# Transposing q by the DMA crossbar, and putting the two attention products of a tile into one burst on TensorE

## The chip, the cores and the metric

The kernel runs on one core of one Trainium2 chip. The metric is the device time of one execution in microseconds (us), as the median of several executions. The kernel before takes 288.21 us (median of 3 runs, 287.4 to 288.27). "Span" below is the time of one profiled execution between its first and its last instruction; it is about 2 us shorter than the device time.

Engine names in the profile: PE is TensorE (matmuls), PEld its weight loads, DVE is VectorE, ACT is ScalarE, POOL is GpSimd, SP is SyncE, which here does nothing but issue DMAs. A "q" after a name (SPq, ACTq) is that engine's instruction queue, as it issues DMAs.

## The reference, cut to what matters

```
q_s = softmax of q over the head dimension         # per row of q
k_s = softmax of k over the sequence               # per column of k
kv  = einsum('bhsd,bhse->bhde', k_s, v)            # k-v product, 64 x 64 per head
att = einsum('bhsd,bhde->bhse', q_s, kv)           # output product
x   = att as [batch * seq, heads * head_dim]       # 4608 x 512
h   = x @ w_in                                     # 512 -> 2048, first matrix product
out = leaky_relu(h) @ w_out                        # 2048 -> 512, second matrix product
```

There are 8 batches of 8 heads, 576 rows of sequence and 64 of head dimension. The two large products are almost all of the work. The kernel goes through x in 9 tiles of 512 rows, which I number 0 to 8. Tile t consists of the first product (64 matmuls of 128x512) and the second (another 64, in four quarters of 16). Attention is prepared ahead: during tile t the kernel finishes batch t+1 and starts on batch t+2.

## The kernel before

Only the parts that the change and the argument touch are shown; `...` marks cuts.

```python
ld_pool = ctx.enter_context(tc.tile_pool(name="ld", bufs=7))
ps_pool = ctx.enter_context(tc.tile_pool(name="ps", bufs=4, space=bass.MemoryType.PSUM))
# pair() takes one of only 4 PSUM tiles of two banks; every matmul result goes to one
...
qe_buf.append(const_pool.tile([P, NG, R * D], BF16, name=f"qe{i}"))     # i = 0, 1
...
def make_transpose(st, b, gp, r0=0, r1=R, copy=None, before=None):      # q on PE
    def piece():
        ...
        pt = pair("pt", BF16)
        for r in range(r0, r1):
            for par, g, lo, to in quads(gp):
                nc.tensor.matmul(
                    pt[to : to + HP, par, r * D : (r + 1) * D],
                    lhsT=qe_buf[b % 2][lo : lo + HP, g, r * D : (r + 1) * D],
                    rhs=ident[lo : lo + HP, lo : lo + HP],
                    is_transpose=True, ...)
        ...
        (copy or nc.vector.tensor_copy)(out=st["qT"][...], in_=pt[...])
...
def prep_pieces(b, st):
    return [
        make_exp(st, b, "q", 0),      # 0  exp on ACT
        make_qnorm(st, b, 0),         # 1  reduce, reciprocal, multiply on DVE
        make_exp(st, b, "q", 1),      # 2
        make_qnorm(st, b, 1),         # 3
        make_exp(st, b, "k", 0),      # 4
        make_exp(st, b, "k", 1),      # 5
        make_vcast(st, b, 0, NG),     # 6  v to bf16 on DVE
    ]
...
# slots: (1, j) runs after column block j (of 16) of the first product,
#        (2, s) after quarter s of the second product
elif t + 1 < B:
    st = states[t + 1]
    put((1, 2), [kv_piece(st, t + 1)] + transpose_pieces(t + 1, st))
    put((1, 8), out_pieces(t + 1))
if t + 2 < B:
    prep = prep_pieces(t + 2, states[t + 2])
    put((2, 0), prep[0:4])
    put((2, 1), prep[4:6])
    put((2, 2), prep[6:7])
...
for t in range(NT):
    if t > 0 and t + 2 < B:
        load_batch(nc.sync, t + 2)          # q, k and v of batch t+2, on SP
    emit_moe(t, slots_of(t))                # its stores are on SP too
```

The order in which these pieces are emitted is the order in which each engine executes its part of them; nothing reorders them later.

The softmax here doesn't subtract the row's maximum and nothing guards it: scores larger than these inputs give would overflow.

## Time and profile before

| | before |
|---|---|
| time, median | 288.21 us |
| span of the profiled run | 285.8 us |
| PE busy | 98% |
| one half of a tile (64 matmuls of 128x512) | 13.81 us, 216 ns each |
| transposes of one batch on PE, tiles 2 to 6 | 0.77 to 0.87 us |
| traffic of the loads falls off, from the start of tile 4 | 15.0 us |
| v's load complete, from the start of tile 2 | 16.7 us |

The first lines of the page, and its line on DMA packets:

```profile
span 285.8 us, 5509 instructions
PE 278.7 (98%) x2484; PEld 130.9 (46%) x2484; DVE 109.5 (38%) x145; ACT 118.8 (42%) x118; POOL 12.8 (4%) x23
...
DMA packets 21894, 42.29 MB, mean 148 GB/s; under 512 B 1776, under 2 KB 6640, under 8 KB 21872
```

PE is busy all the time, and no other engine over half of it. The chain of waits that ended last, in order of time, says the same and shows the pieces. These are its lines for tile 4 (start us, length us, what):

```profile
136.85 2.59 PE ph L376 x12
139.44 0.71 PE pkv L234 x71
140.15 0.77 PE pt L209 x72
140.92 5.29 PE ph L376 x24
146.21 0.61 PE po L280 x16
146.82 6.16 PE ph L376 x28
152.98 13.81 PE pout L385 x64
```

The tile of 29.94 us (136.85 to 166.79) is 27.85 us of the two large products and 2.09 us of attention: k-v product (pkv), transposes of q (pt), output product (po). There is no wait in it.

From the timeline of DVE in the second half of tile 4 (start, length, instruction, and in brackets the idle time before it and who ended it):

```profile
155.13 1.35 DVE L183 TENSOR_REDUCE qsum<-qe 128x18 f32<-128x1152 bf16 x1 [6.69 <-ACT qe L158]
...
158.09 1.34 DVE L183 TENSOR_REDUCE qsum<-qe 128x18 f32<-128x1152 bf16 x1
...
161.04 1.22 DVE L402 COPY out_sb<-pout 128x1024 f32<-128x1024 f32 x1
162.18 1.35 DVE L168 CAST vb<-v_ld 128x2304 bf16<-128x2304 f32 x1
```

Two normalizations of q (each a reduce, a reciprocal and a multiply, which take 2.95 us), then the copy that empties the first pair of output subtiles from PSUM (pout), then the cast of v, last. Roughly when v arrives is seen in the windows (columns: window, length, busy us and count of five engines, clock, DMA share, GB/s), where the load traffic of tile 4 falls off:

```profile
151.00:151.50 0.50, 0.50 (x4) 0.19 (x2) 0.00 (x0) 0.21 (x1) 0.00 (x0) 1.00 0.92 364
151.50:152.00 0.50, 0.50 (x4) 0.24 (x3) 0.00 (x0) 0.50 (x1) 0.00 (x0) 1.00 0.27 101
```

That is 15.0 us after the tile's start at 136.69, about 10 us before the cast that reads v. And these are the loads on SP's queue:

```profile
140.58 0.67 SPq L84 DMA_DIRECT2D q_ld<-in_q_dram  x1
141.34 0.55 SPq L84 DMA_DIRECT2D k_ld<-in_k_dram  x1
141.99 2.11 SPq L84 DMA_DIRECT2D v_ld<-in_v_dram  x1
```

They follow the stores of the tile before, 3.9 us after the tile's start.

### The profile page before, as it was taken

To read this page: it belongs to the slowest core of one execution; us is meant where nothing else is said; L and a number is where in the kernel's file an instruction comes from. 1 tells how busy PE (TensorE), PEld (TensorE's weight loads), DVE (VectorE), ACT (ScalarE), POOL (GpSimd) and SP (SyncE) were. 2 spreads that over 40 slices of the span, in tenths; PEclk is the share of its full clock that TensorE was granted. 3 is DMA by queue.
4 is the path that set the end of the run, shared out by engine and by line. 5 is a ranking of instruction groups with operands and counts; after the bars stand their busy time and mean duration, and the time that the engine had idled before them with its cause. 6 is when DMAs were issued, how large, how long until landed. Compare 5 with 4: busy or idle time off the path is not lost.

```text
span 285.8 us, 5509 instructions
## 1 busy us (share of the span) xinstructions
PE 278.7 (98%) x2484; PEld 130.9 (46%) x2484; DVE 109.5 (38%) x145; ACT 118.8 (42%) x118; POOL 12.8 (4%) x23
## 2 busy tenths in 40 slices
PE   8899999999999999999999999999999999999994
PEld 3344444444454445444544454444444444444443
DVE  2930385919822654246422833092311100110012
ACT  5646444891146703680268116731560065015400
POOL 0832200000000000000000000000000000000000
PEclk9999999999999999999999999999999999999999
DMA  7999999890398036902492149404200330032014
GB/s 260 309 200 246 346 346 402 254 363 5 73 254 320 1 73 152 399 23 66 97 393 92 29 103 337 181 0 99 50 2 0 73 76 0 5 81 63 0 32 114
DMA packets 21894, 42.29 MB, mean 148 GB/s; under 512 B 1776, under 2 KB 6640, under 8 KB 21872
## 3 DMA queue, kind: packets, MB, share of 16 engines
q1 hardware_dynamic: 15312, 30.55, 34.3%
q0 software_dynamic: 6400, 11.27, 15.3%
q8 instruction: 19, 0.31, 0.5%
q10 hardware_dynamic: 160, 0.13, 0.2%
q14 instruction: 3, 0.02, 0.0%
HBM read 36.70 MB, written 9.44 MB: 161 GB/s over the span
## 4 chain that ended last, share of the span: by engine, by line
PE 84%; DMA 13%; POOL 1%; DVE 0%; SPq 0%; issue 0%
PE ph L376 39%; PE pout L385 39%; DMA w_out_sb<-in_moe_w_out_dram 7%; DMA w_in_sb<-in_moe_w_in_dram 4%; DMA k_ld<-in_k_dram 2%; PE pkv L234 2%; PE po L280 2%; PE pt L209 1%; PE pout L414 1%; POOL w_in_sb L116 1%; SPq L84 0%; DVE xT L296 0%; DVE out_sb L422 0%; POOL gate L124 0%
## 5 line engine op out<-in xcount | busy, mean ns | idle before, releaser
L376 PE MATMUL ph<-xT,w_in_sb 128*128 128x512 bf16 x576 | 127.7, 379 | 0.0
L431 ACT ACTIVATE g_sb<-ph 128x1024 bf16<-128x1024 f32 x72 | 73.5, 1023 | 125.1 <-PE ph L376 125.1
L385 PE MATMUL pout<-w_out_sb,g_sb 128*128 128x512 bf16 x560 | 123.4, 379 | 0.3 <-DMA w_out_sb<-in_moe_w_out_dram 0.3
L376 PEld LDWEIGHTS <-w_in_sb 128*128 128x128 bf16 x576 | 55.2, 98 | 66.6 <-issue 1.2
L385 PEld LDWEIGHTS <-g_sb 128*128 128x128 bf16 x560 | 54.4, 98 | 65.8 <-issue 1.0
L402 DVE COPY out_sb<-pout 128x1024 f32<-128x1024 f32 (+1 forms) x18 | 21.4, 1192 | 78.9 <-PE pout L385 76.7
L183 DVE TENSOR_REDUCE qsum<-qe 128x18 f32<-128x1152 bf16 (+2 forms) x18 | 21.9, 1215 | 47.6 <-ACT qe L158 47.6
L296 DVE CAST xT<-po 128x128 bf16<-128x128 f32 (+7 forms) x23 | 13.7, 639 | 28.0 <-PE po L280 27.9
L185 DVE TENSOR_TENSOR qe<-qe,qrec 128x1152 bf16<-128x1152 bf16 (+2 forms) x18 | 22.0, 1225 | 0.6
L158 ACT ACTIVATE ke<-k_ld 128x1152 bf16<-128x1152 f32 x16 | 17.9, 1155 | 4.7 <-DMA k_ld<-in_k_dram 4.7
L158 ACT ACTIVATE qe<-q_ld 128x1152 bf16<-128x1152 f32 x16 | 17.9, 1156 | 3.7 <-DMA q_ld<-in_q_dram 3.7
L219 DVE COPY qT<-pt 128x1152 bf16<-128x1152 bf16 (+1 forms) x16 | 11.3, 740 | 1.1 <-PE pt L209 1.1
L152 PE MATMUL scr<-wsrc 128*128 128x512 bf16 x36 | 10.1, 440 | 1.2 <-DVE wsrc L92 1.2
L296 ACT CAST xT<-po 128x896 bf16<-128x896 f32 (+3 forms) x7 | 5.8, 829 | 12.5 <-PE po L280 12.5
L168 DVE CAST vb<-v_ld 128x2304 bf16<-128x2304 f32 (+2 forms) x8 | 9.6, 1199 | 0.0
L209 PE MATMUL pt<-ident,qe 64*64 64x64 bf16 x568 | 7.6, 196 | 0.5 <-DVE qe L185 0.5
L234 PE MATMUL pkv<-vb,ke 64*64 64x65 bf16 x576 | 6.7, 193 | 0.9 <-ACT vb L168 0.4
L234 PEld LDWEIGHTS <-ke 64*64 64x64 bf16 x576 | 5.7, 106 | 4.1 <-issue 3.3
L209 PEld LDWEIGHTS <-qe 64*64 64x64 bf16 x568 | 6.7, 104 | 1.5 <-issue 1.4
L280 PE MATMUL po<-qT,kd 64*64 64x512 bf16 (+7 forms) x128 | 6.4, 293 | 0.4 <-DVE kd L246 0.4
L152 PEld LDWEIGHTS <-wsrc 128*128 128x128 bf16 x36 | 3.7, 109 | 6.4 <-issue 2.7
L245 DVE RECIPROCAL krec<-pkv 128x4 f32<-128x4 f32 (+1 forms) x9 | 1.6, 178 | 11.2 <-PE pkv L234 11.1
(28 smaller groups left out, 40.1 us busy)
## 6 DMA issues: line engine op xcount, KB each, us to landing
out_dram<-out_sb SPq DMA_DIRECT2D x70, 128.0 KB, 2.4
q_ld<-in_q_dram SPq DMA_DIRECT2D x5, 1152.0 KB, 6.8
k_ld<-in_k_dram SPq DMA_DIRECT2D x5, 1152.0 KB, 8.8
v_ld<-in_v_dram SPq DMA_DIRECT2D x5, 1152.0 KB, 10.8
q_ld<-in_q_dram POOLq DMA_DIRECT2D x2, 1152.0 KB, 18.1
k_ld<-in_k_dram POOLq DMA_DIRECT2D x2, 1152.0 KB, 20.1
v_ld<-in_v_dram POOLq DMA_DIRECT2D x2, 1152.0 KB, 19.8
w_in_sb<-in_moe_w_in_dram POOLq DMA_DIRECT2D x3, 512.0 KB, 10.2
```

The costliest lines, as they stand in the source:

```text
L152: nc.tensor.matmul(scratch["t"][:, 0, :], lhsT=wsrc[:, 0:P], rhs=wsrc, start=True, stop=True)
L158: nc.scalar.activation(out=(qe_buf if nm == "q" else ke_buf)[b % 2][:, 2 * gp : 2 * gp + 2, :], in_=st[nm][:, 2 * gp : 2 * gp + 2, :], fun ...
L183: nc.vector.reduce_sum(out=qsum[:, :, 0:n], in_=x, axis=AX.X)
L185: nc.vector.tensor_tensor(out=x, in0=x, in1=qrec[:, :, 0:n].unsqueeze(3).to_broadcast([P, 2, n, D]), op=ALU.mult,)
L209: nc.tensor.matmul(pt[to : to + HP, par, r * D : (r + 1) * D], lhsT=qe_buf[b % 2][lo : lo + HP, g, r * D : (r + 1) * D], rhs=ident[lo : lo ...
L234: nc.tensor.matmul(pkv[to : to + HP, par, i * VW : i * VW + D + 1], lhsT=ke[lo : lo + HP, g, r * D : (r + 1) * D], rhs=vb[lo : lo + HP, g, ...
L280: nc.tensor.matmul(pos[par % len(pos)][lo : lo + HP, par, at : at + n], lhsT=kd_buf[b % 2][frm : frm + HP, g, :], rhs=states[b]["qT"][frm ...
L296: copies[0](out=dst, in_=pos[0][:, :, at : at + n])
L376: nc.tensor.matmul(ph[:, j % 2, :], lhsT=w_in_sb[:, cb, j * P : (j + 1) * P], rhs=x[:, cb, :], start=(cb == 0), stop=(cb == NB - 1),)
L385: nc.tensor.matmul(pout[:, tsub % 2, :], lhsT=g_sb[:, j, tsub * P : (tsub + 1) * P], rhs=w_out_sb[:, j, :], start=(j == 0), stop=(j == NF ...
L402: nc.vector.tensor_copy(out=out_sb[:, k0:k1, :], in_=pout[:, k0:k1, :])
L431: nc.scalar.activation(out=g_sb[:, 2 * jj : 2 * jj + 2, :], in_=ph, func=AF.Prelu, alpha=LEAKY_SLOPE)
```

## The change

The intent is to take the transposes of q off PE, the engine that bounds the kernel. For batches 2 to 7 they become one crossbar transpose per batch (a DMA that writes its source transposed, DMA_TRANSPOSE in the profile), issued on SP. q's exponentials get a layout that one such DMA can transpose (`[P, R, NG, D]`). As nothing of attention is then left to do between two parts of the first product, the k-v product of batch t+2 and the output product of batch t+1 move to one burst, after three quarters of the second product. For that, v is cast and k exponentiated before q.

```diff
-        qe_buf.append(const_pool.tile([P, NG, R * D], BF16, name=f"qe{i}"))
+        qe_buf.append(const_pool.tile([P, R, NG, D], BF16, name=f"qe{i}"))
...
+    def dma_transpose(st, b):
+        nc.sync.dma_start_transpose(
+            out=qT_of(st).rearrange("c r gp hp p -> c (r gp) (hp p)"),
+            in_=qe_buf[b % 2].rearrange("p r g d -> p (r g d)"),
+        )
...
         if t == 1:
...
+            put((1, 9), [lambda: dma_transpose(st, 2)])
+            put((2, 0), out_pieces(1)[2:3] + [kv_piece(st, 2)])
-            put((2, 0), out_pieces(1)[2:3] + transpose_pieces(2, st) + [kv_piece(st, 2)])
-            outs = out_pieces(2)
-            put((2, 2), outs[0:2])
-            put((2, 3), outs[2:3])
-        elif t + 1 < B:
-            st = states[t + 1]
-            put((1, 2), [kv_piece(st, t + 1)] + transpose_pieces(t + 1, st))
-            put((1, 8), out_pieces(t + 1))
-        if t + 2 < B:
-            prep = prep_pieces(t + 2, states[t + 2])
-            put((2, 0), prep[0:4])
-            put((2, 1), prep[4:6])
-            put((2, 2), prep[6:7])
+        n = t + 2
+        if n < B:
+            prep = prep_pieces(n, states[n])
+            put((1, NF - 1), prep[6:7])
+            put((2, 0), prep[4:6] + prep[0:4])
+            put((2, NTS - 1), [lambda: dma_transpose(states[n], n)])
+        if t + 1 < B:
+            outs = out_pieces(t + 1)
+            put((2, 2), outs[0:1])
+            if n < B:
+                put((2, 2), [kv_piece(states[n], n)])
+            put((2, 2), outs[1:3])
```

Cut: the same change of layout in the exponentials, normalizations and the transposes that stay on PE (batches 0 and 1), a new order of the four 64x64 matmuls of a head pair, and which part of the output product ACT copies. On SP the transpose of batch t+2 stands after the stores of tile t and before the loads of batch t+3.

More of the change, by code (lines that the diff above doesn't have):

```diff
@@ L99 @@
     for i in range(2):
-        qe_buf.append(const_pool.tile([P, NG, R * D], BF16, name=f"qe{i}"))
+        qe_buf.append(const_pool.tile([P, R, NG, D], BF16, name=f"qe{i}"))
         ke_buf.append(const_pool.tile([P, NG, R * D], BF16, name=f"ke{i}"))
         v_buf.append(const_pool.tile([P, NG, R, VW], BF16, name=f"vb{i}"))
-        kd_buf.append(const_pool.tile([P, NG, D], BF16, name=f"kd{i}"))
+        kd_buf.append(const_pool.tile([P, NP, 2, D], BF16, name=f"kd{i}"))
         nc.vector.memset(v_buf[i][:, :, :, D:VW], 1.0)
@@ L157, in piece @@
         def piece():
-            nc.scalar.activation(
-                out=(qe_buf if nm == "q" else ke_buf)[b % 2][:, 2 * gp : 2 * gp + 2, :],
-                in_=st[nm][:, 2 * gp : 2 * gp + 2, :],
-                func=AF.Exp,
-            )
+            gs = slice(2 * gp, 2 * gp + 2)
+            if nm == "q":
+                nc.scalar.activation(
+                    out=qe_buf[b % 2][:, :, gs, :].rearrange("p r g d -> p g r d"),
+                    in_=st[nm][:, gs, :].rearrange("p g (r d) -> p g r d", d=D),
+                    func=AF.Exp,
+                )
+            else:
+                nc.scalar.activation(out=ke_buf[b % 2][:, gs, :], in_=st[nm][:, gs, :], func=AF.Exp)
         return piece
@@ L177, in piece @@
             n = r1 - r0
-            x = qe_buf[b % 2][:, 2 * gp : 2 * gp + 2, r0 * D : r1 * D].rearrange(
-                "p g (r d) -> p g r d", d=D
-            )
-            qsum = small_pool.tile([P, 2, R], FP32, name="qsum")
-            qrec = small_pool.tile([P, 2, R], FP32, name="qrec")
-            nc.vector.reduce_sum(out=qsum[:, :, 0:n], in_=x, axis=AX.X)
-            nc.vector.reciprocal(out=qrec[:, :, 0:n], in_=qsum[:, :, 0:n])
+            x = qe_buf[b % 2][:, r0:r1, 2 * gp : 2 * gp + 2, :]
+            qsum = small_pool.tile([P, R, 2], FP32, name="qsum")
+            qrec = small_pool.tile([P, R, 2], FP32, name="qrec")
+            nc.vector.reduce_sum(out=qsum[:, 0:n], in_=x, axis=AX.X)
+            nc.vector.reciprocal(out=qrec[:, 0:n], in_=qsum[:, 0:n])
             nc.vector.tensor_tensor(
@@ L187, in piece @@
                 in0=x,
-                in1=qrec[:, :, 0:n].unsqueeze(3).to_broadcast([P, 2, n, D]),
+                in1=qrec[:, 0:n].unsqueeze(3).to_broadcast([P, n, 2, D]),
                 op=ALU.mult,
@@ L197, in quads, with qT_of @@
     def quads(gp):
-        for par in range(2):
-            for lo in (0, HP):
-                yield par, 2 * gp + par, lo, (HP - lo if par else lo)
+        for hp in range(2):
+            for par in range(2):
+                yield hp, par, 2 * gp + par, slice(hp * HP, hp * HP + HP), slice(par * HP, par * HP + HP)
+    def qT_of(st):
+        if "qT" not in st:
+            st["qT"] = qT_pool.tile([P, R, NP, 2, D], BF16, name="qT")
+        return st["qT"]
     def make_transpose(st, b, gp, r0=0, r1=R, copy=None, before=None):
         def piece():
-            if "qT" not in st:
-                st["qT"] = qT_pool.tile([P, NG, S], BF16, name="qT")
+            qT = qT_of(st)
             pt = pair("pt", BF16)
             for r in range(r0, r1):
-                for par, g, lo, to in quads(gp):
+                for hp, par, g, hs, ps in quads(gp):
                     nc.tensor.matmul(
-                        pt[to : to + HP, par, r * D : (r + 1) * D],
-                        lhsT=qe_buf[b % 2][lo : lo + HP, g, r * D : (r + 1) * D],
-                        rhs=ident[lo : lo + HP, lo : lo + HP],
+                        pt[ps, hp, r * D : (r + 1) * D],
+                        lhsT=qe_buf[b % 2][hs, r, g, :],
+                        rhs=ident[hs, hs],
                         is_transpose=True,
@@ L219, in piece @@
             (copy or nc.vector.tensor_copy)(
-                out=st["qT"][:, 2 * gp : 2 * gp + 2, r0 * D : r1 * D],
-                in_=pt[:, :, r0 * D : r1 * D],
-            )
-        return piece
+                out=qT[:, r0:r1, gp, :, :].rearrange("c r hp p -> c hp r p"),
+                in_=pt[:, :, r0 * D : r1 * D].rearrange("c hp (r p) -> c hp r p", p=D),
+            )
+        return piece
+    def dma_transpose(st, b):
+        nc.sync.dma_start_transpose(
+            out=qT_of(st).rearrange("c r gp hp p -> c (r gp) (hp p)"),
+            in_=qe_buf[b % 2].rearrange("p r g d -> p (r g d)"),
+        )
     def make_kv(st, b, gps=range(NP)):
@@ L232, in piece @@
                 for r in range(R):
-                    for par, g, lo, to in quads(gp):
+                    for hp, par, g, hs, ps in quads(gp):
                         nc.tensor.matmul(
-                            pkv[to : to + HP, par, i * VW : i * VW + D + 1],
-                            lhsT=ke[lo : lo + HP, g, r * D : (r + 1) * D],
-                            rhs=vb[lo : lo + HP, g, r, 0 : D + 1],
+                            pkv[ps, hp, i * VW : i * VW + D + 1],
+                            lhsT=ke[hs, g, r * D : (r + 1) * D],
+                            rhs=vb[hs, g, r, 0 : D + 1],
                             start=(r == 0),
@@ L242, in finish @@
             def finish():
-                acc = pkv[:, :, 0 : n * VW].rearrange("p par (i e) -> p par i e", e=VW)
+                acc = pkv[:, :, 0 : n * VW].rearrange("p hp (i e) -> p hp i e", e=VW)
                 krec = small_pool.tile([P, 2, n, 1], FP32, name="krec")
@@ L246, in finish @@
                 nc.vector.tensor_tensor(
-                    out=kd[:, 2 * gps[0] : 2 * gps[0] + 2 * n, :].rearrange(
-                        "p (i par) e -> p par i e", par=2
-                    ),
+                    out=kd[:, gps[0] : gps[0] + n, :, :].rearrange("p i hp e -> p hp i e"),
                     in0=acc[:, :, :, 0:D],
@@ L278, in piece @@
                 n = c1 - c0
-                for par, g, lo, frm in quads(gp):
+                for hp, par, g, hs, ps in quads(gp):
                     nc.tensor.matmul(
-                        pos[par % len(pos)][lo : lo + HP, par, at : at + n],
-                        lhsT=kd_buf[b % 2][frm : frm + HP, g, :],
-                        rhs=states[b]["qT"][frm : frm + HP, g, c0:c1],
+                        pos[par % len(pos)][hs, par, at : at + n],
+                        lhsT=kd_buf[b % 2][ps, gp, hp, :],
+                        rhs=states[b]["qT"][ps, c0 // D : c1 // D, gp, hp, :],
                         start=True,
@@ L301, in make_out, with out_pieces @@
         return piece
-    def out_pieces(b):
+    def out_pieces(b, on_act=0):
         n1 = TT - (b * S) % TT
@@ L312, in out_pieces @@
         return [
-            make_out(parts, (nc.scalar.copy if i == 1 else nc.vector.tensor_copy,))
+            make_out(parts, (nc.scalar.copy if i == on_act else nc.vector.tensor_copy,))
             for i, parts in enumerate(groups)
@@ L360, in rest_transpose @@
         for gp in range(NP):
-            for par, g, lo, to in quads(gp):
+            for hp, par, g, hs, ps in quads(gp):
                 nc.tensor.matmul(
-                    pt[to : to + HP, par, gp * D : (gp + 1) * D],
-                    lhsT=qe_buf[0][lo : lo + HP, g, (R - 1) * D : R * D],
-                    rhs=ident[lo : lo + HP, lo : lo + HP],
+                    pt[ps, hp, gp * D : (gp + 1) * D],
+                    lhsT=qe_buf[0][hs, R - 1, g, :],
+                    rhs=ident[hs, hs],
                     is_transpose=True,
@@ L370, in rest_transpose @@
         nc.vector.tensor_copy(
-            out=st["qT"][:, :, TT:S].rearrange("c (gp par) p -> c par gp p", par=2),
-            in_=pt[:, :, 0 : NP * D].rearrange("c par (gp p) -> c par gp p", p=D),
+            out=st["qT"][:, R - 1].rearrange("c gp hp p -> c hp gp p"),
+            in_=pt[:, :, 0 : NP * D].rearrange("c hp (gp p) -> c hp gp p", p=D),
         )
@@ L497, in slots_of @@
             put((2, 12), [make_out([(0, gp, TT, S) for gp in range(NP)]), kv_piece(st, 1)])
-            put((2, 13), out_pieces(1)[0:2])
+            put((2, 13), out_pieces(1, 1)[0:2])
             return slots
```

## The prediction

> **What bounds the kernel now.** TensorE. The page gives PE 98% of a 285.8 us span at full clock. In the chain of waits every 64-matmul half of a token tile takes 13.81 us, and from 46 us on nothing but PE stands in the chain, except 0.77 us of a DVE copy at 63.8. Only work removed from PE, or stalls added to it, moves the time.
>
> **Removed from PE.** The transposes of q. In the chain the 72 transposes of a batch cost 0.87, 0.78, 0.77, 0.80 and 0.78 us in tiles 2 to 6; those of batch 2, in tile 1, about the same (0.81 us in the timeline). Six batches: about 4.7 us. The k-v product (0.71 us) and the output product (0.61 us) only move, from two places in the first matrix product to one burst after three quarters of the second; fewer switches give perhaps 0.2 us.
>
> **Added.** Six crossbar transposes of 128x2304 bf16 (590 KB), one instruction each on SP, ahead of the three loads of the next batch. The Trainium skill, "DMA: Bandwidth & Descriptors", section "Latency and other measured facts", gives 261 GB/s for one kernel's DMA transpose and about 350 to 400 contiguous; from that I estimate 1.6 to 2.3 us each. No run here shows it yet; plain loads reach 400 GB/s in the windows.
>
> **Critical path.** The result itself has over 20 us until it is read. The danger is the queue behind it. Today v of the coming batch lands about 15.2 us after the tile starts (windows). In the new order the second half starts at 13.8 us; k's and q's exponentials follow the last activation (two take 2.21 us), the first q reduce can start 4.4 us into the half, and v's cast (1.35 us, earlier in DVE's order) must be over by then: v has about 1.6 us of slack. DVE then needs 5.9 us for both normalizations and 1.2 us for the copy of the first output pair, which ends 11.5 us into the half; the last output product needs that PSUM pair at about 11.8 us. It just fits. A transpose of 2 us costs tenths of a us per tile; each us beyond is paid in full in tiles 2 to 5. In tile 1 v of batch 3 landed at 63.7 us, and its cast now stands ahead of copies and normalization: a stall of about 1 us.
>
> **Sum.** 288.2 - 4.7 - 0.2 + 1.0 + 0.4 = 284.7; I say 284.5 us, 282.3 to 289.5 for 8 in 10. Chances: faster by over 2% 0.06, within 2% 0.83, slower by over 2% 0.11.
>
> **What would show it.** (1) The transposes fall from 568 to 136 matmuls on the page. (2) In the chain the first half of tiles 2 to 6 is one piece of 13.81 us, and one burst of 1.3 to 1.5 us stands before the last quarter of the second half. (3) Each transpose takes 1.6 to 4 us from issue to landing; the loads behind it land about 2 us later. (4) PE's waits list waits under 0.5 us in tiles 2 to 5, and about 1 us in tile 1, on a DVE copy that frees a PSUM pair. (5) exp, reduce and multiply in the new layout keep 1156, 1350 and 1358 ns.
>
> **What would make it wrong.** A crossbar transpose several times slower than the page says, or a long descriptor issue on SP: with 6 us the stall would be 4 us in each of four tiles and the kernel slower by 3 to 4%. Slower exp or reduce on the interleaved layout would do the same through DVE. If the loads keep enough slack, the time is about 283.

## The result, and the profile after

The changed kernel takes 296.23 us (median of 4 runs, 295.99 to 297.24); before, 287.89 us. It passed the comparison with the reference (e6 below shows how little that says of the transposes), and it is slower: the ratio is 1.0297, with a 95% interval of 1.0266 to 1.0328. (A ratio here is the mean time of one kernel's fast runs over that of the other's fast runs of the same rounds, so it is not quite the ratio of the medians quoted.) The time lies outside the predicted range of 282.3 to 289.5 us.

The first lines of the page of the changed kernel, and its line on DMA packets:

```profile
span 294.5 us, 4646 instructions
PE 277.3 (94%) x2052; PEld 127.7 (43%) x2052; DVE 101.2 (34%) x129; ACT 119.0 (40%) x122; POOL 12.8 (4%) x23
...
DMA packets 35908, 45.78 MB, mean 155 GB/s; under 512 B 15793, under 2 KB 20657, under 8 KB 35889
```

The transposes did leave PE: there are 432 matmuls fewer, which is 6 batches of 72. But PE, busy 98% before, is now busy 94%. The six transposes come with 14,017 more packets under 512 bytes. The chain of waits that ended last, for tile 4, no longer stays on PE:

```profile
141.74 5.20 PE ph L387 x24
...
146.96 1.03 ACT g_sb L442
147.99 1.11 SPq L234
...
149.14 0.59 SPq L84
...
150.33 10.79 DMA v_ld<-in_v_dram
...
161.14 1.36 DVE vb L172
...
168.33 1.23 DVE out_sb L413
...
169.60 0.36 PE po L291 x4
169.96 3.56 PE pout L396 x16
```

Read it from the end. The last part of the output product (po) waited for DVE's copy of the first output pair (out_sb), which set a PSUM pair free. That copy stood in DVE's order behind both normalizations and the cast of v (vb). The cast waited for v's load, the load for its issue on SP, and that issue for the transpose (L234). The chain goes on from there to an activation on ACT, as if the transpose had waited for it. It had hardly done so: the tool names the last update of the awaited semaphore before the instruction's end. In e7 below the transposes start 0.6 us later in their tile and end 0.3 to 0.5 us later, while ACT's activation keeps its place, and the second transposes of e5, with no such wait in the list, hold SP for 2.8 to 3.1 us all the same. The timeline of PE gives the sizes of the waits in the burst of this tile:

```profile
165.85 0.36 PE L291 MATMUL po<-qT,kd 64*64 64x192 bf16 x8
166.03 0.78 PE L247 MATMUL pkv<-vb,ke 64*64 64x65 bf16 x72
167.17 0.36 PE L291 MATMUL po<-qT,kd 64*64 64x384 bf16 x4 [0.35 <-ACT xT L307]
169.60 0.36 PE L291 MATMUL po<-qT,kd 64*64 64x384 bf16 x4 [2.08 <-DVE out_sb L413]
```

The timelines of SP and of DVE, for the same tile, which starts at 141.58:

```profile
145.54 3.56 SPq L234 DMA_TRANSPOSE qT<-qe  x1
149.14 0.59 SPq L84 DMA_DIRECT2D q_ld<-in_q_dram  x1
149.78 0.50 SPq L84 DMA_DIRECT2D k_ld<-in_k_dram  x1
150.33 0.49 SPq L84 DMA_DIRECT2D v_ld<-in_v_dram  x1
```

```profile
161.14 1.36 DVE L172 CAST vb<-v_ld 128x2304 bf16<-128x2304 f32 x1 [18.14 <-DMA v_ld<-in_v_dram]
162.42 1.35 DVE L185 TENSOR_REDUCE qsum<-qe 128x18 f32<-128x1152 bf16 x1
...
168.33 1.22 DVE L413 COPY out_sb<-pout 128x1024 f32<-128x1024 f32 x1
```

The transpose holds SP for 3.56 us. The loads are issued 7.6 us after the tile's start instead of 3.9, and v's load is complete 19.5 us after it. In the kernel before that was 16.4 in this tile, counted in the same way; over tiles 2 to 5 the means are 19.0 and 16.5. From there DVE needs 1.28 + 5.91 + 1.22 us to the end of the copy, and PE waits. Over all tiles, the list of PE's waits (total us, times, longest) has

```profile
PE po L291 <- DVE out_sb L413: 7.8, 5, 2.3
PE po L291 <- ACT xT L307: 1.4, 4, 0.6
```

which is 9.2 us, where PE had waited 0.2 us in all after tile 0 before. Something else comes on top. After the waits of tiles 1 and 5 the clock of PE is at half speed for about 3.4 us; the windows of tile 1 (after five busy times: clock, DMA share, GB/s) and the 16 matmuls that follow the burst in tiles 1 and 4, from PE's timeline:

```profile
76.00:77.00 1.00, 1.00 (x4) 0.45 (x3) 0.99 (x3) 0.00 (x0) 0.00 (x0) 0.50 0.93 209
77.00:78.00 1.00, 1.00 (x4) 0.31 (x3) 0.00 (x0) 0.00 (x0) 0.00 (x0) 0.50 0.84 201
```

```profile
75.00 5.31 PE L396 MATMUL pout<-w_out_sb,g_sb 128*128 128x512 bf16 x16
...
169.89 3.63 PE L396 MATMUL pout<-w_out_sb,g_sb 128*128 128x512 bf16 x16
```

The same 16 matmuls take 5.31 us in place of 3.63; with tile 5 that is 2 x 1.68 = 3.4 us.

The account: 9.2 us of new waits and 3.4 us of slow clock, less 4.7 us of transposes removed, is 7.9 us. The spans differ by 8.7 us, of which another 0.36 us was lost before tile 1 began. Some 0.4 us stays unaccounted for.

### The profile page after: what moved, and what is told of

It reads as the page before. It is cut to its first block, busy times and chain, and to the rows that moved or that the text cites. A ratio compares the mean times of both kernels' runs of the same rounds, so it can differ in the third digit from the quotient of the medians.

```text
span 294.5 us, 4646 instructions
## 1 busy us (share of the span) xinstructions
PE 277.3 (94%) x2052; PEld 127.7 (43%) x2052; DVE 101.2 (34%) x129; ACT 119.0 (40%) x122; POOL 12.8 (4%) x23
## 4 chain that ended last, share of the span: by engine, by line
PE 47%; DMA 31%; DVE 13%; issue 3%; SPq 3%; ACT 2%; POOL 1%; DVEq 0%
PE ph L387 23%; PE pout L396 21%; DMA v_ld<-in_v_dram 18%; DMA w_out_sb<-in_moe_w_out_dram 7%; DVE qsum L185 4%; DMA w_in_sb<-in_moe_w_in_dram 3%; DVE qe L187 3%; DVE vb L172 2%; DMA k_ld<-in_k_dram 2%; DVE out_sb L413 2%; SPq L84 2%; ACT g_sb L442 1%; PE pout L425 1%; PE po L291 1%; DVE qrec L186 1%
## 5 line engine op out<-in xcount | busy, mean ns | idle before, releaser
L396 PE MATMUL pout<-w_out_sb,g_sb 128*128 128x512 bf16 x560 | 127.6, 386 | 0.6 <-DMA w_out_sb<-in_moe_w_out_dram 0.6
L387 PE MATMUL ph<-xT,w_in_sb 128*128 128x512 bf16 x576 | 126.0, 379 | 0.0
L387 PEld LDWEIGHTS <-w_in_sb 128*128 128x128 bf16 x576 | 56.3, 98 | 67.7 <-issue 0.2
L166 ACT ACTIVATE ke<-k_ld 128x1152 bf16<-128x1152 f32 x16 | 17.9, 1156 | 10.5 <-DMA k_ld<-in_k_dram 10.5
L160 ACT ACTIVATE qe<-q_ld 128x1152 bf16<-128x1152 f32 x16 | 17.9, 1151 | 4.0 <-DMA q_ld<-in_q_dram 4.0
L307 ACT CAST xT<-po 128x512 bf16<-128x512 f32 (+6 forms) x11 | 5.4, 529 | 34.7 <-PE po L291 34.7
L291 PE MATMUL po<-qT,kd 64*64 64x512 bf16 (+7 forms) x128 | 8.0, 296 | 9.8 <-DVE out_sb L413 7.8
L307 DVE CAST xT<-po 128x896 bf16<-128x896 f32 (+7 forms) x19 | 14.0, 781 | 3.6 <-PE po L291 3.6
L291 PEld LDWEIGHTS <-kd 64*64 64x64 bf16 x128 | 3.2, 104 | 15.9 <-issue 14.4
L186 DVE RECIPROCAL qrec<-qsum 128x18 f32<-128x18 f32 (+2 forms) x18 | 4.6, 254 | 0.6
L119 POOL DMA_DIRECT2D w_out_sb<-in_moe_w_out_dram x5 | 3.8, 767 | 3.7 <-DMA w_in_sb<-in_moe_w_in_dram 3.7
L116 POOL DMA_DIRECT2D w_in_sb<-in_moe_w_in_dram x5 | 3.9, 795 | 0.0
```

The source lines that it names most:

```text
L160: nc.scalar.activation(out=qe_buf[b % 2][:, :, gs, :].rearrange("p r g d -> p g r d"), in_=st[nm][:, gs, :].rearrange("p g (r d) -> p g r ...
L166: nc.scalar.activation(out=ke_buf[b % 2][:, gs, :], in_=st[nm][:, gs, :], func=AF.Exp)
L291: nc.tensor.matmul(pos[par % len(pos)][hs, par, at : at + n], lhsT=kd_buf[b % 2][ps, gp, hp, :], rhs=states[b]["qT"][ps, c0 // D : c1 // D ...
L307: copies[0](out=dst, in_=pos[0][:, :, at : at + n])
L387: nc.tensor.matmul(ph[:, j % 2, :], lhsT=w_in_sb[:, cb, j * P : (j + 1) * P], rhs=x[:, cb, :], start=(cb == 0), stop=(cb == NB - 1),)
L396: nc.tensor.matmul(pout[:, tsub % 2, :], lhsT=g_sb[:, j, tsub * P : (tsub + 1) * P], rhs=w_out_sb[:, j, :], start=(j == 0), stop=(j == NF ...
```

## The experiments

**Theory T (queue).** A crossbar transpose on SP, ahead of the loads, makes v late; v's cast stands in DVE's order before the copy that frees the PSUM pair of the burst; so PE waits. **Rival S (schedule):** the new order of the work is too tight by itself, with or without the DMA. **Rival B (bandwidth):** crossbar traffic slows the loads wherever it stands. **Rival D:** crossbar transposes cost PE time by themselves.

Eight kernels were run, in two jobs of four; each was timed in three rounds beside the kernel before, which took 287.52 us in the first job and 287.55 us in the second, so that medians of both can be compared.

| run | what it is | median us | ratio to before [95%] | v lands after tile start, tile 2, us |
|---|---|---|---|---|
| (the change) | | 296.23 | 1.0297 [1.0266, 1.0328] | 18.7 |
| e1_loads_first | transpose after the loads | 286.46 | 0.9963 [0.9924, 1.0002] | 15.4 |
| e2_act_queue | transpose on ACT's queue | 285.53 | 0.9946 [0.9906, 0.9987] | 15.5 |
| e3_pe_transposes | new order, transposes on PE | 292.27 | 1.0162 [1.0146, 1.0178] | 16.8 |
| e4_old_schedule | old order, transposes on SP | 285.71 | 0.9940 [0.9921, 0.9959] | not waited for |
| e5_twice | each transpose twice | 315.04 | 1.0957 [1.0909, 1.1005] | 22.3 |
| e6_plain_copy | plain copy in its place | 287.34 | 1.0004 [0.9956, 1.0052] | 16.5 |
| e7_late_norm | second normalization later | 283.80 | 0.9871 [0.9848, 0.9894] | 19.5 |
| e9_old_act | old order, transposes on ACT's queue | 282.88 | 0.9843 [0.9828, 0.9857] | not waited for |

(There is no e8. The last column is the start of v's cast on DVE where DVE waited for v.)

One caution for that column. With nothing in front of the loads, v's load is complete after 15.3 to 16.1 us in tiles 2 to 5 of e1 and e2, but after 16.0 to 16.9 us in the kernel before and in e3, and in two tiles of e9 only after 17.7 and 17.8. No run shows why. So "how much the transpose delays v" depends on what it is counted from: 3.4 us from e2, 2.5 us from the kernel before or from e3. The issue of the first load does not have this uncertainty: it comes 3.9 to 4.4 us after the tile's start in e1, e2 and e3, and 6.7 to 7.6 us in the change, on average 3.0 us later than in e2.

### e1: the loads first

```diff
-            put((2, NTS - 1), [lambda: dma_transpose(states[n], n)])
...
             load_batch(nc.sync, t + 2)
+        if 2 <= t and t + 1 < B:
+            dma_transpose(states[t + 1], t + 1)
         emit_moe(t, slots_of(t))
```

> Edit: the transpose of batches 3 to 7 is issued after the three loads of the next batch instead of before them; all else as in the changed kernel. Theory T (queue): the transpose instruction holds SP for 2.6 to 3.6 us and everything behind it, so v lands 18.7 us after the tile starts instead of 15.2, and DVE's chain (cast, two normalizations, copy of the first output pair) ends too late for the last output product. Then v lands at about 15 us here, the waits of PE in tiles 2 to 5 (0.2+1.5, 0.6+0.5, 0.4+2.1, 2.3 us) fall under 1 us in all, the slow clock of tile 5 goes too, tile 1 keeps its wait: about 288.5 us. Rival S (schedule): the new order is too tight by itself, whatever the DMA queue does: stays near 296 us. Rival B (bandwidth): crossbar traffic slows the loads wherever it stands: v lands at 17 us or later, 291 to 296 us.

Measured: 286.46 us, 9.8 us faster than the change. v lands 15.4 us after the start of tile 2, and PE's waits in tiles 2 to 5 come to 0.6 us (0.21, 0.18 and 0.23 us). That is what T said of the stalls (the time is 2 us under the one I expected), and it speaks against S and B for those tiles: the same order and the same traffic, behind the loads, cost next to nothing. Tile 1 keeps its waits, 0.29 + 1.72 us. The spread is telling: two of the four runs had a mean clock of 1.0 and took 285.26 and 285.61 us, the other two 0.991 and 0.994 and took 287.72 and 287.32 us. In the profiled one (clock 1.0) the 16 matmuls after tile 1's wait took 3.63 us. So the slow clock comes in some executions and not in others, and costs about 2 us where it does; that it follows the same wait of tile 1 there is likely, but the two slow-clocked runs have no trace. One more thing is in the trace: behind the loads, the transposes hold SP for 9.4 to 10.0 us, in place of 2.6 to 3.6, and land 12.0 us after their issue (median of six). So the hold is no fixed cost of the instruction. It did no harm, as SP had nothing else to issue in that time.

### e2: ACT's queue

```diff
-    def dma_transpose(st, b):
-        nc.sync.dma_start_transpose(
+    def dma_transpose(st, b, eng=nc.sync):
+        eng.dma_start_transpose(
...
-            put((2, NTS - 1), [lambda: dma_transpose(states[n], n)])
+            put((2, NTS - 1), [lambda: dma_transpose(states[n], n, nc.scalar)])
```

> Edit: the transposes of batches 3 to 7 are issued from ACT's queue at the same place of the program, so SP goes on to the loads. Theory T: SP issues the loads some 2.7 us earlier, v lands near 15.5 us after the tile starts, PE's waits in tiles 2 to 5 fall under 1.5 us in all, about 288.5 us, as with the loads first. ACT has over 4 us of idle time there, so its sequencer being held for 3 us costs nothing. Rival B (bandwidth): the transfers still compete, v lands at 17 us or later, 291 to 296 us. Rival S (schedule): 296 us.

Measured: 285.53 us, 3 us under what I expected; v lands at 15.5 to 15.7 us in tiles 2 to 5, PE's waits there are 0.6 us, tile 1 keeps 0.29 + 1.78 us. ACT's queue issues each transpose in 2.5 to 4.2 us, where ACT has nothing to do. The Trainium skill, "Trainium Kernel Development and Optimization", section "Key Constraints", says that issuing from several engines only saves the sequencer's issue time; that time, about 3 us here, was the point. The run does not separate it cleanly from bandwidth, as ACT's queue also starts the transpose some 10 us earlier, well before the loads (73.5 us in tile 1 of this run, 84.1 us in the change). e6 does that better.

### e3: the new order with the transposes on PE

```diff
-            put((1, 9), [lambda: dma_transpose(st, 2)])
-            put((2, 0), out_pieces(1)[2:3] + [kv_piece(st, 2)])
+            put((2, 0), out_pieces(1)[2:3] + transpose_pieces(2, st) + [kv_piece(st, 2)])
+        elif t + 1 < B:
+            put((1, 2), transpose_pieces(t + 1, states[t + 1]))
...
-            put((2, NTS - 1), [lambda: dma_transpose(states[n], n)])
```

> Edit: the new order of the work with no crossbar transpose at all: q of batches 2 to 7 is transposed on PE again (batch 2 in tile 1, the others after two column blocks of the first product of the next tile, where they were before), the common burst stays. Theory T: loads are not delayed, waits of PE in tiles 2 to 5 vanish, tile 1 has about 1 us of wait left: 288 to 289.5 us. Rival S (schedule): the order alone costs the waits of 9 us, and PE has its 4.7 us of transposes back: 298 to 301 us.

Measured: 292.27 us, between what T and S expected. The trace says where it lies. In tiles 2 to 5 PE's waits are 0.6 us in all, so S falls for those tiles: without the DMA in front of the loads the burst fits. In tile 1, however, the k-v product waited 2.48 us for a DVE copy of a PSUM pair, which stood in DVE's order behind the cast of v of batch 3, and the 32 matmuls after it took 8.77 us instead of 7.08 (the windows show a clock of 0.51 just then). Those two make 4.2 us. For tile 1 the rival is right: the new order alone, with v's cast ahead of the copies, makes PE wait there, and I had allowed it 1 us. (It is not quite the wait of the change: e3 also has batch 2's transposes and their two copies at this spot, and its wait falls on the k-v product, that of the change on the output product later on.)

### e4: the old order with the transposes on SP

```diff
-            put((1, NF - 1), prep[6:7])
-            put((2, 0), prep[4:6] + prep[0:4])
+            put((2, 0), prep[0:4])
+            put((2, 1), prep[4:6])
+            put((2, 2), prep[6:7])
             put((2, NTS - 1), [lambda: dma_transpose(states[n], n)])
-        if t + 1 < B:
-            outs = out_pieces(t + 1)
-            put((2, 2), outs[0:1])
-            if n < B:
-                put((2, 2), [kv_piece(states[n], n)])
-            put((2, 2), outs[1:3])
+        ... (cut: k-v product at (1, 2) and output product at (1, 8), as before the change)
```

> Edit: only the transposes move to the crossbar, in the same place of SP's queue as in the changed kernel (before the loads); the k-v product, the output product, the exponentials and the cast of v keep the places that they had before the change. Theory T: v lands as late as in the changed kernel (18 to 19 us after the tile starts), but here its cast stands last in DVE's order and nothing on PE waits for it in that tile: no PE wait over 0.3 us in tiles 2 to 5, 283 to 284.5 us, faster than before by some 4.5 us. Rival D: crossbar transposes cost PE by themselves, in any order: 288 us or more.

Measured: 285.71 us, so rival D falls: the crossbar takes 1.8 us off the kernel when the order is the old one. But it missed my range, which was 283 to 284.5. The waits for DVE are gone, as expected, though v's load is complete only 19.2 to 20.5 us after the start of tiles 2 to 5; and a new one is there, which I had not thought of:

```profile
PE po L291 <- DMA qT<-qe: 2.4, 4, 0.7
```

In the old order the output product comes in the middle of the next tile's first half, and the transposed q, issued after the stores, is 0.4 to 0.7 us too late for it.

### e5: each transpose twice

```diff
+    twice = const_pool.tile([P, R, NP, 2, D], BF16, name="twice")
+    def dma_transpose_twice(st, b):
+        dma_transpose(st, b)
+        nc.sync.dma_start_transpose(out=twice..., in_=qe_buf[b % 2]...)
...
-            put((2, NTS - 1), [lambda: dma_transpose(states[n], n)])
+            put((2, NTS - 1), [lambda: dma_transpose_twice(states[n], n)])
```

> Edit: the changed kernel with each transpose of batches 3 to 7 issued twice in the same place before the loads, the second into a tile that nobody reads. Theory T (queue): one transpose costs the loads behind it 3 to 3.5 us, so v lands another 2.7 to 3.5 us later (about 22 us after the tile starts) and each of tiles 2 to 5 stalls about 3 us more: 12 us more in all, with the slow clock after longer stalls 1.7 us a time: 308 to 314 us. If the transpose were cheap and the stalls came from elsewhere, the time would stay within 2 us of 296.

Measured: 315.04 us, 18.8 us slower than the change (I expected 12 to 18). v lands on average 22.0 us after the start of tiles 2 to 5 (22.3, 21.1, 22.1, 22.4), against 19.0 in the change (18.7, 18.2, 19.5, 19.5): 3.0 us for one more transpose. PE's waits on the copy rise from 7.8 to 20.7 us, and the slow clock now follows the burst in tiles 1 to 5 (4.90 to 6.06 us for the 16 matmuls that should take 3.63). SP's timeline, in tile 3 of this run:

```profile
121.20 2.89 SPq L234 DMA_TRANSPOSE qT<-qe  x1
124.13 2.76 SPq L243 DMA_TRANSPOSE twice<-qe  x1
126.99 0.53 SPq L84 DMA_DIRECT2D q_ld<-in_q_dram  x1
```

One more transpose moved the first load's issue by 2.8 us and v by 3.0 us, and PE paid for it: that is the strongest evidence for the first link of T. Of the 18.8 us, 12.9 are longer waits on the copy and 5.9 slow clock.

### e6: a plain copy in its place

```diff
+    def plain_copy(st, b):
+        nc.sync.dma_start(out=qT_of(st)..., in_=qe_buf[b % 2]...)
...
-            put((2, NTS - 1), [lambda: dma_transpose(states[n], n)])
+            put((2, NTS - 1), [lambda: plain_copy(states[n], n)])
```

> Edit: the transposes of batches 3 to 7 are replaced by a plain copy of the same 590 KB from SBUF to SBUF in the same place of SP's queue; the result is wrong on purpose. It tells the transport of the bytes from what is special to the transpose. If moving 590 KB is what delays the loads, it delays them about as much and the time stays at 293 to 297 us. If the long issue on SP (2.6 us and more) and the low rate of the crossbar are what counts, SP is held 0.5 to 0.6 us, the copy takes 1.5 to 2 us at the 400 GB/s of plain loads, v lands at 16.5 to 17.5 us, and about 288 to 290 us result.

(The comparison with the reference passed even so; q is nearly uniform after its softmax, so the comparison hardly sees the order of q: shuffling q along the sequence in batches 2 to 7 moves the reference's own output by 0.15% (relative norm, worked out with the reference on a CPU). So a passed comparison does not show that the crossbar transposes of the change and of the other versions are right, either; no run here does. The edit copies q without transposing it, and its output is not to be used.) Measured: 287.34 us, a little under my 288 to 290. SP is held 0.53 us per copy:

```profile
141.90 0.53 SPq L240 DMA_DIRECT2D qT<-qe  x1
```

v lands at 16.5, 16.6, 17.1 and 17.7 us in tiles 2 to 5. Against e2, where nothing stands before the loads (15.5 to 15.7 us), the plain copy costs them 1.4 us on average and the transpose 3.4 us; against e3 it is 0.4 and 2.5 us. Either way the bytes are less than half of it, and the transpose costs 2.0 us more than the copy. Most of that lies in the hold of SP: behind the copy the first load is issued 0.6 us later than in e2, behind the transpose 3.0 us, while from issue to landing the two differ by only 1.0 us (medians of 3.8 and 4.8). Why the transpose holds SP so long, a slow transfer among the possible reasons, is not shown.

### e7: the second normalization later

```diff
-            put((2, 0), prep[4:6] + prep[0:4])
-            put((2, NTS - 1), [lambda: dma_transpose(states[n], n)])
+            put((2, 0), prep[4:6] + prep[0:3])
+            states[n]['norm1'] = prep[3]
...
     for t in range(NT):
+        if 2 <= t and t + 1 < B:
+            states[t + 1]['norm1']()
+            dma_transpose(states[t + 1], t + 1)
         if t > 0 and t + 2 < B:
             load_batch(nc.sync, t + 2)
```

> Edit: only DVE's order changes. The second normalization of q stands after the copies of tile t (at the head of tile t+1, just before the transpose, which is still before the loads), no longer before the copy that frees the first output pair. Theory T's second link says that the late v hurts only through that copy: v lands as late as in the changed kernel or later (19 to 20 us), yet the copy ends 3 us earlier in DVE's order and PE's waits on it vanish in all of tiles 1 to 5 (under 0.5 us each): 283.5 to 286 us. If PE waited for something else that is late (the transposed q, the loads themselves), the time stays near 296 us.

Measured: 283.80 us, 12.4 us faster than the change, with the transposes still on SP ahead of the loads. DVE's timeline in tile 4, which starts at 134.89:

```profile
154.66 1.36 DVE L172 CAST vb<-v_ld 128x2304 bf16<-128x2304 f32 x1 [15.38 <-DMA v_ld<-in_v_dram]
...
158.89 1.22 DVE L413 COPY out_sb<-pout 128x1024 f32<-128x1024 f32 x1
...
165.58 1.34 DVE L185 TENSOR_REDUCE qsum<-qe 128x18 f32<-128x1152 bf16 x1
```

v lands 19.8 us after the start, later even than in the change (19.5), but now only 2.95 us of normalization stand between its cast and the copy, and PE waits 0.7 us in all after tile 0 (0.4 for ACT, 0.3 for that copy). The wait of tile 1 is gone as well, and so is the slow clock: the four runs had clocks of 0.998 to 1.0. This is the second link of T: the late v hurts only through the place of the copy in DVE's order.

### e9: the old order, transposes on ACT's queue

```diff
 (from e4)
-            put((2, NTS - 1), [lambda: dma_transpose(states[n], n)])
+            put((2, 2), [lambda: dma_transpose(states[n], n, nc.scalar)])
```

> Edit: the order of the work of before, transposes of batches 3 to 7 by the crossbar from ACT's queue right after the second normalization (over 4 us before the end of the tile), so that neither the loads nor the output product waits. The run with the order of before and the transposes on SP had 2.4 us of PE waits on the transposed q; these should go: 283 to 284 us, 1.3 to 1.6% faster than before, no slow clock. It also tells what the common burst is worth: if merging the two products saved PE time, this version would be slower than the one with the burst and ACT's queue (285.5 us with its 2 us wait in tile 1); I expect it to be faster by about 2 us.

Measured: 282.88 us (282.74 to 283.54), just under what I expected. PE waits for nothing after tile 0, and ACT's queue issues the transpose in a gap of its own:

```profile
128.59 2.71 ACTq L234 DMA_TRANSPOSE qT<-qe  x1
```

This is the fastest version, 1.6% faster than the kernel before and 4.5% faster than the change (282.88 against 296.23 us). The gain over before, 287.55 - 282.88 = 4.7 us, is the whole of what the transposes of six batches cost on PE. The common burst shows no gain: e7, which keeps it, is 0.9 us slower, about as much as its 0.7 us of waits.

## Why the prediction was wrong, point by point

- **"Six batches: about 4.7 us" off PE: right.** 432 matmuls are gone, and e9 gets 4.7 us out of that.
- **"The danger is the queue behind it": right in mechanism.** Late loads, late cast, late copy, PE waiting for a PSUM pair: the chain of waits shows each link, and e1, e5 and e7 confirm them one at a time. The deadline was right too: the prediction's numbers have v due by about 16.8 us after the tile's start, with 0.3 us to spare behind it. In all eight tiles 2 to 5 of the change and of e5, v's landing less PE's waits gives 17.1 to 17.2 us.
- **"I estimate 1.6 to 2.3 us each": this is the step that failed.** The estimate came from a bandwidth on a page of the Trainium skill, "DMA: Bandwidth & Descriptors", section "Latency and other measured facts". Measured, a transpose holds SP for 2.6 to 3.6 us in tiles 2 to 6, takes 4.8 us from issue to landing, and puts the first load 3.0 us later (2.8 us for one more of them in e5). With 15.2 us for v today and 2 us more, v was to land at about 17.2 us, just at the deadline; it landed at 18.2 to 19.5 us, on average 19.0. The stalls of tiles 2 to 5 were 1.67, 1.06, 2.43 and 2.31 us, on average 1.87, instead of tenths. So the term "0.4" of the sum measured 7.5 us.
- **"v has about 1.6 us of slack": right or wrong by what one counts from.** The 15.2 us were read from the windows, where the traffic falls off. Counted by completion, as for the other runs, v was there after 16.1 to 16.8 us in the kernel before, and the slack was some 0.6 us; in e1 and e2 it was 1.0 to 1.8 us. How much of the 1.87 us of stall is a dearer transpose and how much a slack read too large stays open.
- **"Each us beyond is paid in full": right**, as the constant 17.1 to 17.2 us above show. The prediction even had the right case in its last paragraph (a long issue on SP), but gave it 11%. That it spoke of 3 to 4% slower there is luck: it had that from 6 us per transpose, and without the slow clock.
- **"A stall of about 1 us" in tile 1: too small.** It was 1.72 us. It belongs to the new order rather than to the crossbar: without any crossbar transpose tile 1 waited 2.48 us (e3, at a place nearby), and the old order with the same crossbar transpose in tile 1 did not wait there (e4, e9).
- **The slow clock was missing from the sum altogether.** Two stretches at half clock cost 3.4 us. They stand right after waits of PE, though not after every one (tile 4 waited 2.4 us and kept full clock); versions without such waits (e7, e9) have none of it. That it follows from the waits is argued from this, not from a run that switches it alone.
- **"Fewer switches give perhaps 0.2 us": not seen.** Less their listed waits, tiles 2 to 5 take 29.2 us on average both in e7, with the burst, and in e9, with the two products apart. In e9 tile 4 takes 29.17 us (134.02 to 163.19), just what the old tile of 29.94 us is without its 0.77 us of transposes.
- **"exp, reduce and multiply in the new layout keep 1156, 1350 and 1358 ns": right** (1151 to 1156, 1347 and 1358 ns).

With the measured terms the sum is 287.9 - 4.7 + 7.5 + 1.7 + 3.4 = 295.8 us, against 296.23 measured.

## What to carry to other kernels

When work moves from a busy engine to a DMA, ask first what stands behind it in the same queue and how much slack that has: here the moved work had 20 us to spare and the loads behind it under 2. Put it behind the loads (if the queue can bear the long hold there, 9.4 to 10.0 us in e1), or on the queue of an engine that is idle at that moment, and keep the copy that sets PSUM free ahead of anything in its engine's order that can wait. A slack that just fits should be priced with a measured duration of the new instruction, and short waits on TensorE with more than their own length, as half clock may follow them.

## What the Trainium skill lacked or had wrong

- "Advanced Engine Details and Errata", section "X-Bar Transpose (TRN2)", says that transpose DMAs are as fast as regular DMAs. For 590 KB from SBUF to SBUF they are not: v landed 2.0 us later behind the transpose than behind a plain copy in the same place (19.0 against 17.0 us after the tile's start), and from issue to landing the transpose took 4.8 us and the copy 3.8 us.
- "DMA: Bandwidth & Descriptors", section "Latency and other measured facts", gives 261 GB/s for one kernel and 350 to 400 for the contiguous case. One more transpose of 590 KB delayed the loads by 3.0 us. As a rate that would be about 197 GB/s (an estimate from this delay, which may not be how the page measured); the source rows and the destination are contiguous in each partition here.
- No page gives, for a size like this one, how long a transpose instruction holds the queue that issues it (the sequencer times of "DMA: Bandwidth & Descriptors" stand in its part on trn3 and are for other sizes): 2.6 to 3.6 us for 128x2304 bf16 in tiles 2 to 6, but 8.0 us in tile 1 and 9.4 to 10.0 us in e1, where loads were still in flight; a plain copy held it 0.53 us.
- "TensorE: Matmul & The Clock Gate", section "Why this matters for your kernels", warns of idle gaps over about 3 us. In the changed kernel half clock followed gaps of 1.7 us (two waits with a short burst between) and 2.3 us, and lasted long enough to add 1.7 us to the next 16 matmuls. It did not follow every such gap: tile 4 of the same run kept full clock after 2.4 us (two waits), and the profiled run of e6 after 2.3 us in tile 1. What decides is not shown.
